# Every second output tile of an attention and gated-MLP kernel goes to the two tiles of the MLP's rectified values

## The chip, the cores and the metric

The kernel runs on one core of one Trainium2 chip. The metric is the device time of one execution in microseconds (us). Engines are named as in the profile: PE is TensorE's matmuls, PEld its weight loads, DVE is VectorE, ACT is ScalarE, POOL is GpSimd, SP is SyncE. A "q" behind a name is that engine's queue of issued instructions, for SP that of its transfers.

## What is computed

For 8 batches of 8 heads, attention with a decay over 576 positions of 64 values, and on its output (8 x 576 x 512) a gated MLP whose gate mixes positions:

```
decay  = cum[:, :, :, None] - cum[:, :, None, :]        # cum = cumsum(log(clip(f)))
attn   = softmax(where(causal, -1e9, q k^T / 8 + decay))
x      = (attn v), heads side by side                   # B x 576 x 512
h      = relu(x @ w_in);  u, v = h[..., :512], h[..., 512:]
v_n    = (v - mean(v)) / sqrt(var(v) + 1e-6)
gated  = u * (w_spatial @ v_n + b_spatial)              # over the 576 positions
out    = gated @ w_out                                  # B x 576 x 512
```

## The kernel before

The work is done in float32 precision on float32r operands: nearly every operand is kept as a high part and a rest, and a product is three (or two) matmuls. Attention (`attention`) goes through 32 pairs of heads, four to a batch; the MLP (`moe`) goes through the 8 batches. The main loop steps both generators side by side, attention a quarter of a batch and more ahead, so that a list of both in alternation is recorded. A scheduler that plans on modelled times then sets each engine's own order; every engine runs its list in order. A change that shifts one instruction can therefore shift everything planned behind it.

A batch of the MLP has these stages. For five groups of tokens (L532 to L570): sum `ps` of 12 matmuls, relu to the tile `vx` (L556, two buffers), mean and variance, the normalised value (L561), its high part `vnh` (ACT) and rest `vnl` (POOL). Then (L574 to L585) eight sums to the tiles `u`. Then for two halves of the tokens (L589 to L612) four gate sums `ps<-sph,vnh`, `spl,vnh`, `sph,vnl`, each multiplied by `u` on DVE and split in `gh` and `gl`. After each half, two output tiles of 128 tokens (`w_out_tile`, L620); after every odd batch a fifth one, with the 64 last tokens of two batches.

`w_out_tile` sums 12 matmuls with `wo` to a `ps` tile, copies it to an SBUF tile and issues its transfer to memory (256 KB) on SP's queue, for the fifth tile half of it on ACT's:

```
tag, bufs = ("vx", 2) if b == B - 1 and nps[0] % 3 else ("o", 1)
o = (mo if tag == "vx" else m2[0]).tile([128, DM], F32, name="o", tag=tag, bufs=bufs)
...
    A.copy(o, ps)
for bb, tok, p0, np_ in dst:
    (A if p0 else SY).dma_start(out=out[bb, tok:tok + np_, :], in_=o[p0:p0 + np_, :])
```

The tag names the buffers that a tile takes in turn. There is one buffer "o", so a copy to it waits until the transfer of the tile before it has read it. "vx" has two. In the last batch (`b == B - 1`) two of three tiles take "vx" already. In the sums, `ps` has two accumulators (the last batch also takes those of attention's scores `sc` and transposes `tp`, two each), so the third sum waits until the first is copied or multiplied away.

SP's queue also carries the loads of attention: for each head of a pair six (L312 to L317, `ta` and `tb`), the values (L323) and the raw queries and keys (L287). In attention, score tiles `sc` (`qkt`) are read by DVE (L357, with the row minimum), exponentiated on ACT (L359), scaled on POOL (L370), transposed on PE to `tp` (L416, L429), and cast from there by ACT to `eh` (L405) and by DVE to the rest `el` (L406); `x` are the products with the values.

Of the kernel before, what the change touches and what calls it, by code (L numbers as in the profile page):

```python
# [38 lines left out]
def attn_gmlp_kernel(ctx: ExitStack, tc: tile.TileContext, qk, v, f, w_in, w_sp, b_sp, w_out, out):  # L39
# [7 lines left out]
    B = out.shape[0]  # L47
# [101 lines left out]
    def after(i, mark, wait=False):  # L149
        if mark in last:  # L150
            tc.add_manual_dep(i.ins, last[mark].ins.name, mybir.DependencyInfo(
                mybir.DependencyClass.Sync if wait else mybir.DependencyClass.NoSync,
                mybir.DependencyReason.DATA), reason="order")
# [117 lines left out]
    def mm(o, l, r, st, sp):  # L271
        last['mm'] = T.matmul(o, l, r, start=st, stop=sp)  # L272
        return last['mm']
# [247 lines left out]
    nps = [0]  # L521

    def acc(b):

        nps[0] += 1
        pool, tag = ((ps_m, "ps"), (PS["t"], "tp"), (PS["s"], "sc"))[nps[0] % 3 if b == B - 1 else 0]
        return pool.tile([128, DM], F32, name=tag)

    def moe(b):
# [59 lines left out]
        for t0, nt in HALVES:  # L589
            gh, gl = [], []  # L590
            for j in range(NJ):
                ps = acc(b)
                o = ps[:, 0:nt]
                js = slice(128 * j, 128 * j + 128)
                for c in range(NB):
                    mm(o, vh[c][:, js], sph[c][:, t0:t0 + nt], c == 0, False)
                    mm(o, vh[c][:, js], spl[c][:, t0:t0 + nt], False, False)
                    mm(o, vl[c][:, js], sph[c][:, t0:t0 + nt], False, False)
                    yield 370
                mm(o, vh[NB][:, js], spta[:, t0:t0 + nt], False, False)  # L600
                mm(o, vb_[:, js], sptb[:, t0:t0 + nt], False, True)
                yield 246
                g = us[j, t0][:, 0:nt]
                V.tensor_tensor(out=g, in0=o, in1=g, op=ALU.mult)
                gh.append(m2[0].tile([128, 320], F32R, name="gh", tag="GH", bufs=3))
                gl.append(m2[0].tile([128, 320], F32R, name="gl", tag="U", bufs=9))
                A.copy(gh[j][:, 0:256], g[:, 0:256])  # L607
                G.tensor_tensor(out=gl[j][:, 0:256], in0=g[:, 0:256], in1=f32(gh[j][:, 0:256]), op=ALU.subtract)  # L608
                if t0:
                    th, tlo = (gt[0][:, r, j, r0:r0 + 64] for r in range(2))  # L610
                    A.copy(th, g[:, 256:320])
                    G.tensor_tensor(out=tlo, in0=g[:, 256:320], in1=f32(th), op=ALU.subtract)  # L612
            for c0 in (0, 128):
                yield from w_out_tile(b, [g[:, c0:c0 + 128] for g in gh], [g[:, c0:c0 + 128] for g in gl],
                                      [(b, t0 + c0, 0, 128)])
        if b % 2 == 1:
            yield from w_out_tile(b, *[[gt[0][:, r, j, :] for j in range(NJ)] for r in range(2)],
                                  [(b - 1, TL, 0, 64), (b, TL, 64, 64)])

    def w_out_tile(b, ghi, glo, dst):  # L620
        ps = acc(b)
        n = 0
        for j in range(NJ):
            for l, r in ((ghi, 0), (ghi, 1), (glo, 0)):
                i = mm(ps, l[j], wo[j][:, r, :], n == 0, n == 3 * NJ - 1)
                n += 1
                if b == B - 1 and n > 6:
                    after(i, "last")
            yield 648
        tag, bufs = ("vx", 2) if b == B - 1 and nps[0] % 3 else ("o", 1)  # L630
        o = (mo if tag == "vx" else m2[0]).tile([128, DM], F32, name="o", tag=tag, bufs=bufs)
        last["last"] = i
        if b == B - 1 and len(dst) == 1:
            V.tensor_copy(o, ps)
        else:
# [3 lines that stand above are left out]
# [94 lines left out]
```

## Time and profile before

| | |
|---|---|
| Median of 3 runs | 787.94 us (785.98 to 788.37) |
| The profiled execution | 786.43 us, of which the profile's span is 784.6 us |
| PE, PEld busy | 771.4 us (98%), 699.8 us (89%) |
| DVE, ACT, POOL busy | 553.1, 541.3, 470.9 us |
| DMA | 103.48 MB in 41713 packets |
| Output tiles | 40 transfers of them, 32 copies on ACT, 4 on DVE |

A row of the timeline reads: start and length in us, engine, line of the program, operation, output tile <- input tiles, shapes, number of instructions merged (x2), and in brackets the idle time of the engine just before it with what ended it. The waits table gives for each pair of engine, tile and line: us in total, times, the longest. PE's matmuls overlap, so a row's length is not the distance to the next one.

### The profile page before, as it was taken

The page shows a single profiled execution, that of the slowest core. Times are in us where ns is not written, and L with a number is a line of the kernel's source. Part 1 is how long each engine was busy: PE and PEld are TensorE (multiplying, and loading weights), DVE is VectorE, ACT ScalarE, POOL GpSimd, SP SyncE. Part 2 cuts the span into 40 slices and gives each one's busy share as a digit, 9 for nine tenths or more (in the row PEclk, how much of TensorE's full clock was granted, in tenths as well). Part 3 has the DMA queues.
Part 4 walks back from the last instruction along what each step waited for, and adds up shares of the span by engine and source line. Part 5 has one row for each costly group of instructions (what it writes and reads, how often), then busy time and mean ns, then how long its engine had stood idle before and what let it go on. Part 6 is the DMA issues. An engine that isn't in the chain of part 4 may idle for free.

```text
span 784.6 us, 15517 instructions
## 1 busy us (share of the span) xinstructions
PE 771.4 (98%) x4979; PEld 699.8 (89%) x4979; DVE 553.1 (70%) x1668; ACT 541.3 (69%) x1444; POOL 470.9 (60%) x687
## 2 busy tenths in 40 slices
PE   9998999999999999999999999999999999999997
PEld 4777889898999889998999989989899989999996
DVE  7989798867677587676766767776677768764422
ACT  8898697766866577667776768766686767764431
POOL 4666787858744476664755666555766547643241
PEclk9999999999999999999999999999999999999999
DMA  9848654654536644564565544556444665320001
GB/s 248 230 147 207 180 160 114 152 148 131 121 92 163 181 124 121 125 161 132 126 147 140 155 132 100 147 148 170 127 108 106 158 171 146 82 64 14 28 1 68
DMA packets 41713, 103.48 MB, mean 132 GB/s; under 512 B 6831, under 2 KB 8879, under 8 KB 41568
## 3 DMA queue, kind: packets, MB, share of 16 engines
q1 hardware_dynamic: 41306, 101.96, 50.9%
q8 instruction: 40, 0.66, 0.4%
q10 hardware_dynamic: 326, 0.53, 0.2%
q14 instruction: 41, 0.34, 0.1%
HBM read 39.42 MB, written 10.68 MB: 64 GB/s over the span
## 4 chain that ended last, share of the span: by engine, by line
PE 90%; DVE 3%; DMA 2%; POOL 2%; ACT 1%; issue 1%; ACTq 0%; POOLq 0%; DVEq 0%
PE ps L272 46%; PE sc L272 17%; PE x L272 13%; PE tp L416 9%; PE tp L429 2%; PE tp L272 2%; DMA out_dram<-o 2%; DVE tt L357 1%; POOL vnl L564 0%; DVE el L406 0%; ACT o L636 0%; POOL lo L292 0%; DVE xl L467 0%; DVE xl L465 0%; DMA ft<-in_dram 0%
## 5 line engine op out<-in xcount | busy, mean ns | idle before, releaser
L370 POOL TENSOR_SCALAR tt<-tt,sm 128x128 f32<-128x128 f32 (+1 forms) x228 | 126.5, 573 | 89.2 <-DVE sm L363 75.3
L357 DVE CUSTOM_DVE_ANT_0 tt<-sc,zm 128x128 f32<-128x128 f32 (+3 forms) x256 | 123.0, 485 | 71.5 <-PE tp L416 48.2
L405 ACT CAST eh<-tp 128x512 fp32r<-128x512 f32 (+1 forms) x270 | 112.4, 424 | 78.1 <-PE tp L416 41.4
L359 ACT ACTIVATE tt<-tt,nm 128x128 f32<-128x128 f32 (+3 forms) x256 | 144.4, 565 | 21.0 <-DVE nm L357 19.7
L406 DVE TENSOR_TENSOR el<-tp,eh 128x512 fp32r<-128x512 f32 (+1 forms) x270 | 129.1, 486 | 39.3 <-ACT eh L405 37.2
L416 PE MATMUL tp<-ident,tt 128*128 128x128 f32 x640 | 113.4, 278 | 0.8 <-DVE el L406 0.6
L292 POOL TENSOR_TENSOR lo<-raw,hi 128x320 fp32r<-128x320 f32 (+1 forms) x112 | 95.3, 881 | 26.0 <-ACT hi L290 25.3
L272 PE MATMUL sc<-ta 128*128 128x128 f32 (+1 forms) x336 | 107.6, 326 | 1.8 <-DVE wa L169 0.9
L272 PE MATMUL sc<-tb 68*128 68x128 f32 (+1 forms) x336 | 104.7, 318 | 2.0 <-DVE ef L401 1.3
L272 PE MATMUL x<-eh,vt 128*128 128x320 f32 (+4 forms) x378 | 105.1, 288 | 0.1
L272 PE MATMUL ps<-xh,win 128*128 128x256 f32 (+1 forms) x464 | 99.1, 301 | 0.0
L608 POOL TENSOR_TENSOR gl<-u,gh 128x256 fp32r<-128x256 f32 x64 | 47.8, 748 | 82.6 <-ACT gh L607 82.3
L272 PE MATMUL x<-el,vt 128*128 128x256 f32 x324 | 92.1, 303 | 0.0
L272 PE MATMUL ps<-win,xh 128*128 128x512 f32 x296 | 90.5, 396 | 0.0
L416 PEld LDWEIGHTS tp<-ident,tt 128*128 128x128 f32 x640 | 76.5, 141 | 8.2 <-PE sc L272 1.2
L272 PEld LDWEIGHTS ps<-xh,win 128*128 128x128 f32 x464 | 75.6, 189 | 0.5
L272 PEld LDWEIGHTS x<-eh,vt 128*128 128x128 f32 x378 | 71.0, 189 | 3.2 <-DVE xl L467 0.2
L272 PE MATMUL ps<-sph,vnh 128*128 128x256 f32 (+1 forms) x240 | 72.5, 302 | 1.3 <-ACT o L636 1.3
L272 PE MATMUL ps<-spl,vnh 128*128 128x256 f32 (+1 forms) x240 | 72.0, 300 | 0.0
L272 PE MATMUL ps<-sph,vnl 128*128 128x256 f32 (+1 forms) x240 | 71.2, 297 | 0.0
L272 PE MATMUL ps<-wo,gh 128*128 128x512 f32 x224 | 69.6, 401 | 1.0 <-ACT wo L178 1.0
L272 PEld LDWEIGHTS sc<-ta 128*128 128x128 f32 x336 | 63.7, 190 | 6.4 <-DVE nm L357 1.4
(177 smaller groups left out, 1898.1 us busy)
## 6 DMA issues: line engine op xcount, KB each, us to landing
raw<-in_dram SPq DMA_DIRECT2D x28, 608.0 KB
ta<-hi SPq DMA_DIRECT2D x56, 304.0 KB
vraw<-in_dram SPq DMA_DIRECT2D x32, 320.0 KB
tb<-hi SPq DMA_DIRECT2D x56, 160.0 KB
ta<-lo SPq DMA_DIRECT2D x56, 160.0 KB
out_dram<-o SPq DMA_DIRECT2D x32, 256.0 KB
ta<-hi SPq DMA_DIRECT2D x56, 144.0 KB
tb<-lo SPq DMA_DIRECT2D x56, 144.0 KB
```

The source lines that it names most:

```text
L272: last['mm'] = T.matmul(o, l, r, start=st, stop=sp)
L292: G.tensor_tensor(out=lo[:, c], in0=raw[:, c], in1=f32(hi[:, c]), op=ALU.subtract)
L357: V.tensor_tensor_reduce(out=t, in0=sc[:, 0:n], in1=zm[:, 640 - n:640], scale=-0.125, scalar=3.0e38, op0=ALU.add, op1=ALU.min, accum_out=n ...
L359: last["exp"] = last["exp", P, h, i] = A.activation(t, t, AF.Exp, bias=nm[:, i:i + 1], scale=-1.0, accum_out=se[:, i, 0:1])
L370: G.tensor_scalar(out=t, in0=t, scalar1=sm[:, i:i + 1], scalar2=1.0, op0=ALU.mult, op1=ALU.mult)
L405: A.copy(h_ap, ps)
L406: V.tensor_tensor(out=l_ap, in0=ps, in1=f32(h_ap), op=ALU.subtract)
L416: T.transpose(out=tp[:, (i - c) * 128:(i - c + 1) * 128], in_=tt[h][:, TOFF[i] + 128 * c:TOFF[i] + 128 * c + 128], identity=ident)
L429: T.transpose(out=tp[:, j * 128:(j + 1) * 128], in_=tl[:, c * 128:(c + 1) * 128], identity=ident)
L608: G.tensor_tensor(out=gl[j][:, 0:256], in0=g[:, 0:256], in1=f32(gh[j][:, 0:256]), op=ALU.subtract)
```

## The change

Ahead of the last batch, an output tile takes "vx" if the number of its token group (its first token by 128: 0 to 3, and 4 for the fifth tile) plus the number of the batch is even. So of the pairs of tiles in an even batch the first one goes to "vx" and the second to "o", in an odd batch the first to "o" and the second to "vx", and the fifth tile of an odd batch to "o". The last batch is as it was.

```
-        tag, bufs = ("vx", 2) if b == B - 1 and nps[0] % 3 else ("o", 1)
+        tag, bufs = ("vx", 2) if (nps[0] % 3 if b == B - 1 else (dst[0][1] // 128 + b) % 2 == 0) else ("o", 1)
```

Each engine has the same instructions as before. Up to the copy of the first output tile the orders are the same, then nearly all differ until the last batch's end. The first place is ScalarE at the first pair of output tiles of the third batch (b = 2): o_4785 and o_4844 are the two tiles, ps_4744 and ps_4788 their sums, eh the casts of transposed tiles, tt the exponentials. Before, around the second copy; the first one stands fourteen instructions ahead of it:

```order
L607 CAST gh_4871<-u_4311 128x256
L611 CAST gt_4532<-u_4311 128x64
L405 CAST eh_1231<-tp_4579 128x512
L359 ACTIVATE tt0_67,se2_99<-tt0_67,nm_4618 128x128
L464 CAST xh_4384<-x1_4515 64x320
L333 CAST vt_4560<-vraw_4558 128x5x2x64
L405 CAST eh_1231<-tp_4597 128x384
L359 ACTIVATE tt0_67,se2_99<-tt0_67,nm_4618 128x256
L636 COPY o_4844<-ps_4788 128x512
L516 CAST xh_4384<-xl_4385 128x64
```

And now, with both copies:

```order
L405 CAST eh_1231<-tp_4326 128x3x2x64
L405 CAST eh_1231<-tp_4335 128x2x2x64
L386 ACTIVATE tl_93,sm_4354<-tl_93,nm_4353 128x576
L636 COPY o_4785<-ps_4744 128x512
L636 COPY o_4844<-ps_4788 128x512
L405 CAST eh_1231<-tp_4431 128x512
L359 ACTIVATE tt1_68,se1_98<-tt1_68,nm_4468 128x128
L405 CAST eh_1231<-tp_4444 128x384
L464 CAST xh_4384<-x1_4387 64x320
```

The second copy has moved up to the first one, ahead of the casts and exponentials that stood between. On SP the two transfers of these tiles (rows `out_dram<-o`) stood behind the loads of both heads of the next pair, and now stand behind those of the first head alone.

The second place is TensorE in the same batch, at the sums to `u` (ps<-xh,win). sc_3952, sc_3974 and sc_4014 are score tiles, of which the third takes the accumulator of the first. Before:

```order
L272 MATMUL ps_4397<-xl_2731,win6_852 128x256
L272 MATMUL ps_4397<-xh_3063,win6_852 128x256 x2
L272 MATMUL ps_4397<-xl_3064,win6_852 128x256
L272 MATMUL ps_4397<-xh_3407,win6_852 128x256 x2
L272 MATMUL ps_4397<-xl_3408,win6_852 128x256
L416 MATMUL tp_3933<-ident_70,tt0_67 128x128
L272 MATMUL x0_4053<-eh_1231,vt_3882 128x256
L272 MATMUL x0_4053<-el_1232,vt_3882 128x256
L272 MATMUL x0_4053<-eh_1231,vt_3882 128x128
L272 MATMUL x0_4053<-el_1232,vt_3882 128x128
L272 MATMUL sc_4014<-ta_3885 128x288
L272 MATMUL sc_4014<-tb_3886 128x288
```

And now:

```order
L272 MATMUL sc_3952<-ta_3885 128x384
L272 MATMUL sc_3952<-tb_3886 128x384
L272 MATMUL sc_3974<-ta_3885 128x512
L272 MATMUL sc_3974<-tb_3886 128x512
L416 MATMUL tp_3925<-ident_70,tt0_67 128x128 x2
L272 MATMUL sc_4014<-ta_3885 128x288
L272 MATMUL sc_4014<-tb_3886 128x288
L272 MATMUL sc_4014<-ta_3893 128x288
L272 MATMUL sc_4014<-tb_3894 128x288
```

The sum ps_4397 (twelve products of 256 columns) and the products x0 that stood between sc_3974 and sc_4014 have gone elsewhere; two products and two transposes are left between the end of sc_3952 and its accumulator's next use.

## Rows read from the trace of the kernel before

**Rows 1.** The page, part 1 (busy us, share of the span, instructions of each engine), and of part 2 the granted clock of TensorE in 40 slices, in tenths of full speed (9 is 90% or more).

```profile
PE 771.4 (98%) x4979; PEld 699.8 (89%) x4979; DVE 553.1 (70%) x1668; ACT 541.3 (69%) x1444; POOL 470.9 (60%) x687
...
PEclk9999999999999999999999999999999999999999
```

**Rows 2.** The table by stretches, six from 160 to 753 us, of which two are shown: stretch, its length, busy us of PE, PEld, DVE, ACT and POOL (with instructions), granted clock, DMA share, GB/s; and the sum over all six.

```profile
330.00:350.00 20.00, 19.11 (x134) 18.23 (x134) 14.40 (x47) 15.29 (x44) 11.12 (x17) 1.00 0.70 176
...
520.00:530.00 10.00, 8.92 (x62) 8.42 (x61) 8.13 (x25) 7.44 (x23) 5.29 (x8) 1.00 0.57 143
...
sum 593.00, PE 590.87 PEld 551.47 DVE 409.91 ACT 403.65 POOL 349.07; mean PE 98.48 PEld 91.91 DVE 68.32 ACT 67.27 POOL 58.18
```

**Rows 3.** The table of waits over the whole span (who waited for whom: us in total, times, longest), and of the view of tile o the row of ACT's copies (ns: shortest, median, longest).

```profile
ACT eh L405 <- PE tp L416: 41.4, 47, 2.7
ACT o L636 <- DMA out_dram<-o: 23.0, 13, 3.6
PEld ps L272 <- ACT o L636: 1.7, 2, 0.9
PE ps L272 <- ACT o L636: 1.3, 2, 0.7
PE sc L272 <- DMA tb<-rows_d: 0.4, 1, 0.4
...
L636 ACT COPY o<-ps x32: 573/587/592, 151.6 to 780.4; 128x512 f32<-128x512 f32 x32
```

**Rows 4.** The timeline around the first pair of output tiles of the third batch: the longest of the loads on SP, the transfers, the two copies, and the next gate sum on PE. The transfers' row merges two, of which the first is issued at its start.

```profile
333.71 0.57 ACT L636 COPY o<-ps 128x512 f32<-128x512 f32 x1
...
334.85 1.17 SPq L314 DMA_DIRECT2D ta<-hi  x1
...
338.06 5.65 SPq L638 DMA_DIRECT2D out_dram<-o  x2
...
342.75 0.59 ACT L636 COPY o<-ps 128x512 f32<-128x512 f32 x1 [0.48 <-DMA out_dram<-o]
...
343.39 0.41 PE L272 MATMUL ps<-sph,vnh 128*128 128x320 f32 x1 [0.65 <-ACT o L636]
```

**Rows 5.** The timeline at the same place of the fifth batch: the gate sum's first product.

```profile
528.58 0.41 PE L272 MATMUL ps<-sph,vnh 128*128 128x320 f32 x1 [0.67 <-ACT o L636]
```

**Rows 6.** The timeline in the fourth batch, first pair: gate products on PE while ACT waits, and the second copy.

```profile
426.92 0.31 PE L272 MATMUL ps<-sph,vnl 128*128 128x320 f32 x1
...
427.06 0.31 PE L272 MATMUL ps<-spta,vnh 128*128 128x320 f32 x1
...
429.65 0.30 PE L272 MATMUL ps<-sph,vnh 128*128 128x320 f32 x1
...
429.80 0.31 PE L272 MATMUL ps<-spl,vnh 128*128 128x320 f32 x1
...
430.00 0.59 ACT L636 COPY o<-ps 128x512 f32<-128x512 f32 x1 [3.15 <-DMA out_dram<-o]
```

**Rows 7.** The timeline at the second pair of the fourth batch: a transfer's issue on SP, and the copy that waits for it.

```profile
448.59 0.37 SPq L638 DMA_DIRECT2D out_dram<-o  x1
...
451.21 0.59 ACT L636 COPY o<-ps 128x512 f32<-128x512 f32 x1 [0.97 <-DMA out_dram<-o]
```

**Rows 8.** The timeline at the second pair of the third batch: the copies, and the second relu of the next batch.

```profile
360.62 0.59 ACT L636 COPY o<-ps 128x512 f32<-128x512 f32 x1
...
364.83 0.59 ACT L636 COPY o<-ps 128x512 f32<-128x512 f32 x1 [0.53 <-DMA out_dram<-o]
...
368.78 0.61 ACT L556 ACTIVATE vx<-ps 128x512 f32<-128x512 f32 x1
```

**Rows 9.** The timeline around a score tile of 384 columns in the second batch: what follows its second product on PE (the first row starts as that product ends), and DVE's reading of it (two instructions).

```profile
262.95 0.28 PE L272 MATMUL x<-eh,vt 128*128 128x256 f32 x1
...
263.07 0.38 PE L416 MATMUL tp<-ident,tt 128*128 128x128 f32 x2
...
263.21 0.36 PE L272 MATMUL x<-el,vt 128*128 128x256 f32 x1
...
263.41 0.39 PE L272 MATMUL sc<-ta 128*128 128x512 f32 x1
...
263.49 0.56 DVE L357 CUSTOM_DVE_ANT_0 tt<-sc,zm 128x384 f32<-128x384 f32 x1 [0.22 <-PE tp L416]
...
263.88 0.23 PE L272 MATMUL x<-eh,vt 128*128 128x128 f32 x1
...
263.97 0.09 DVE L357 DVE_READ_ACCUMULATOR2_ANT nm<- 128x1 f32 x1
```

**Rows 10.** The groups of instructions by line and shape: two neighbouring kinds of product of one shape (busy us, mean ns of one, idle before).

```profile
L272 PE MATMUL x<-eh,vt 128*128 128x320 f32 x162 | 51.5, 324 | 0.1
L272 PE MATMUL x<-el,vt 128*128 128x320 f32 x162 | 49.8, 315 | 0.0
```

**Rows 11.** The chain of waits in order of time: start, us, what; the pieces that are transfers of output tiles, the longest ones.

```profile
263.19 3.69 DMA out_dram<-o
268.30 3.49 DMA out_dram<-o
...
338.06 4.62 DMA out_dram<-o
...
523.18 4.69 DMA out_dram<-o
```

## The prediction

> **What bounds the kernel now.** I read the engines' busy times first. TensorE is busy for 771.4 of 784.6 us, no other engine for more than 553.1, and its granted clock is at full speed in every slice [rows 1]. Then the table by stretches, because a mean hides where the rest lies. From 160 us, shortly after the first two output tiles, to 753 us, TensorE is busy for 590.87 of 593.00 us [rows 2]: it is idle for 2.13 us, and nearly all of that lies in 330 to 350 us (0.89) and in 520 to 530 us (1.08). The rest of its 13.2 us of idle time lies in the start and the last 30 us, which the change doesn't reach. So TensorE's own list of work sets the end, and what a change of buffers can return is what stands idle in those two places.
>
> Third, the table of waits. ScalarE stands 23.0 us before 13 copies of output tiles because the one tile "o" is still being written to memory; but TensorE waits for such a copy only twice, 1.3 us by its matmuls and 1.7 us by its weight loads [rows 3]. Fourth, the instructions around one of the two places [rows 4]. The first copy of the pair ends at 334.28. Its transfer to memory is issued at 338.06, since SP first works through six loads of attention's, the longest of them 1.17 us. The second copy starts at 342.75, and TensorE, which has no accumulator free for the next gate product, starts that at 343.39 after 0.65 us of idle time. The same pattern gives 0.67 us at 528.58 [rows 5]. Elsewhere the wait is longer and costs nothing: before 430.00 ScalarE waits 3.15 us, and TensorE's gate products follow each other every 0.15 us through all of it [rows 6].
>
> **The change part by part.**
>
> What it removes. The second copy of a pair no longer waits for the first one's transfer. No instruction is added or taken away: the copies stay 32 on ScalarE of 587 ns (median) [rows 3], the transfers keep their number and size, and TensorE's matmuls are the same. Of the 23.0 us of ScalarE's waiting, the two places are on the path, with the 1.7 us by which weight loads wait there [rows 3]. The other eleven waits I cost at nothing. What hides them is TensorE's other work, which is attention's products for the pairs ahead; if that cover were gone (it is in the last batch, whose tiles the change leaves as they are) they would cost up to 3.6 us each. The bounds of this term: at least 1.3 us (by the matmuls' waits), at most 2.13 us, TensorE's whole idle time from 160 to 753 us. **Term 1: -1.7 us.**
>
> That gain hangs on a slow transfer. From its issue to the next copy's start a transfer takes 4.69 us in the place at 338.06, and 2.62 us at 448.59 [rows 4, 7]. The Trainium skill, page "DMA: Bandwidth & Descriptors", section on the two cost components, says that a transfer costs about 2 us fixed and then its bytes at 436 GB/s; for these 256 KB that is an estimate of 2.6 us. It agrees with the quicker row and not with the slower one; were all transfers like that, the second copy would be ready 2.1 us earlier, there would be no stall to remove, and the sum would end 1.7 us higher. The stall is measured, so I keep the rows.
>
> What it moves. The copies of a pair now stand side by side on ScalarE and the transfers side by side on SP, mostly ahead of the second set of loads instead of behind it. The casts behind them (eh) start up to 0.59 us later. Their cover is large: ScalarE itself waits 41.4 us for TensorE before those casts [rows 3], so I cost this at nothing, which is the end that these rows are nearest to; the far end, 13 x 0.59 = 7.7 us with the cover gone in every place, belongs to the slower rival below. For SP, a load that stands behind a transfer must now wait for the copy; the bound from the trace is the one wait of TensorE for such a load, 0.4 us [rows 3]. I take nothing, as loads that stood behind the first transfer now stand behind two that are ready together.
>
> What it adds: a wait on the tile "vx". The two buffers alternate, and the first relu of the next batch takes the buffer that was free, the second takes the one that the last such output tile used. The tightest boundary is from an even batch. In batch 2 the copy that will use vx is the one at 360.62 and the second relu comes at 368.78, 8.16 us later; the hold lasts until the transfer is through, at 364.8, or 4.2 us after the copy's start [rows 8]. So 4 us are to spare and I cost it at nothing. In the slow place of [rows 4] the hold was 9.0 us, which would leave ScalarE waiting 0.9 us at three such boundaries, 2.6 us together, and TensorE has a second accumulator to cover it.
>
> What it does beside this: after the first pair of output tiles nearly every engine's order is another one, as the scheduler plans on from there. TensorE's list has the same matmuls in other places, and some stand closer to what they wait for. The place shown above in the order: a score tile (288 columns) follows the one of 384 columns that used its accumulator after only two products of 512 columns and two transposes. By the trace those take 0.47 + 0.14 us, and from the end of a 384-column score product (262.95) to the end of VectorE's reading of it (264.06) pass 1.11 us [rows 9]: 0.5 us short. The next tightest place that I found is short by some 0.2 us. Before, the first of them had twelve products of 256 columns and more in between. **Term 2: +0.7 us.** Bounds: 0 (VectorE's reading may come earlier, as it sat idle only 0.22 us there) and one such stall of 0.5 us in each of the seven batches that move, 3.5 us.
>
> **The sum.** The profiled execution took 786.43 us, its span 784.6 us. 786.43 - 1.7 + 0.7 = 785.4 us. That execution is 1.5 us below the median of the runs (787.94 us), so in terms of the median the forecast is **786.9 us**, a change of -0.13%. About 0.3%, 2.4 us, is what a measurement of this kernel can tell from no change. With the bounds of both terms the forecast's own range is 787.94 - 2.13 = 785.8 to 787.94 - 1.7 + 3.5 = 789.7 us.
>
> **The rivals.**
>
> *Denser products.* TensorE's rows overlap (a product of 320 columns is shown as 0.31 us and the next one starts after 0.15 us), so that short stalls hide inside "busy". With another order some 3800 products could each follow a little more closely. A mere 1 ns each gives 3.8 us, hence 787.94 - 1.7 - 3 = 783.3 us with most of that. For it: products of one form differ in mean by 9 ns between neighbours in the order (324 and 315 ns) [rows 10]. Against it: the scheduler's order was not made for that, and the number of changes between kinds of products is nearly the same in both orders. Chance 0.21.
>
> *The waits at face value.* The chain of waits passes four times through a transfer of an output tile, 3.69 + 3.49 + 4.62 + 4.69 = 16.5 us [rows 11]. If that time came back, 787.94 - 16.5 = 771.4 us would be left. The Trainium skill speaks for looking this way: its page "Perfetto Trace Analysis", section on the most-contended engine, calls TensorE's busy share a poor measure of the room that is left and wants the busy share of weight loads instead. That share is 89% here [rows 1], which by that page leaves room. What speaks against it in this trace is [rows 6]: during the longest such waits the products come at their usual distance, and a chain that runs through a transfer says nothing of TensorE's other work at that moment. Chance 0.05.
>
> *Accumulators turned over too fast* (slower). The place is score tiles and transpose tiles on TensorE in the new order, the mechanism that of term 2: products planned before VectorE or ScalarE have emptied the accumulator, which in-order TensorE can't pass. At 0.5 us each it decides from nine places on (9 x 0.5 - 1.7 = 2.8 us). With two in each of seven batches it is 7.0 us, thus 787.94 - 1.7 + 7.0 = 793.2 us. For it: the order shows more pairs of score tiles close to each other than before, and VectorE and ScalarE are busy for some 70% of the time [rows 1]. Against it: I found two such places, not nine. Chance 0.19.
>
> That the change does nothing is not a case: the order shows the copies side by side.
>
> **How the numbers follow.** Forecast 0.55 (within 0.3%), faster 0.21 + 0.05 = 0.26, slower 0.19. The range from 783.3 to 790.3 takes in the forecast, most of the denser order and the mild part of the slower rival; it leaves out the waits at face value and the 793 us end.
>
> **What would show it.** Right: no wait of ScalarE's copies for a transfer but a rest of a few us, where an odd batch's fifth tile uses "o" again; no idle TensorE before the gate product in the third and fifth batch; TensorE idle between 160 and 753 us for 1 to 3 us in other places, after score or transpose tiles; a relu's wait for a transfer absent. Wrong: a span shorter by over 2.4 us with the same idle time would speak for denser products; idle TensorE of over 4 us behind VectorE's reading of scores for the slower rival; relus that wait for a transfer would mean that I misjudged the hold of "vx".

## The result: slower by one per cent, and the profile after

The changed kernel takes 794.64 us (median of 6 runs, 792.83 to 796.58), the kernel before 786.56 us beside it (6 runs, 784.87 to 788.37): a ratio of **1.0102, 95% interval 1.0078 to 1.0126**, 8.1 us slower. The forecast was no change. Times of all kernels below are medians; ratios are to the kernel before, timed beside each on the same chip. The profiled executions of two kernels (a_ob and rev_parity, below) were disturbed ones, and nothing is read from their traces.

The profiled execution after took 794.53 us, its span 792.7 us. Part 1 of its page, and the clock of part 2:

```profile
PE 777.1 (98%) x4978; PEld 702.1 (89%) x4979; DVE 553.6 (70%) x1668; ACT 542.8 (68%) x1444; POOL 469.2 (59%) x687
...
PEclk9999999999999999999999999999999999999999
```

Against [rows 1] TensorE is busy for 5.7 us more with the same work, and the total of VectorE, ScalarE or GpSimd has moved by 1.7 us at most. A slice of part 2 is 19.8 us long, so that its 9 can hide a fall of the clock that lasts a few us. The table by stretches, from 160 us to where the same work ends in this order (761 us); columns as in [rows 2]:

```profile
160.00:330.00 170.00, 169.08 (x1125) 156.36 (x1124) 118.62 (x369) 118.67 (x320) 102.93 (x158) 1.00 0.52 130
330.00:350.00 20.00, 20.00 (x139) 19.31 (x138) 13.67 (x41) 12.52 (x37) 12.65 (x22) 1.00 0.63 154
350.00:386.00 36.00, 35.42 (x215) 31.23 (x214) 26.24 (x85) 25.36 (x66) 22.09 (x37) 1.00 0.60 150
386.00:396.00 10.00, 8.47 (x52) 8.14 (x51) 7.24 (x21) 7.21 (x19) 5.61 (x9) 0.83 0.39 89
...
570.00:590.00 20.00, 19.16 (x136) 17.48 (x136) 16.03 (x50) 16.07 (x42) 15.62 (x24) 1.00 0.71 171
...
sum 601.00, PE 596.60 PEld 553.62 DVE 411.61 ACT 407.20 POOL 348.64; mean PE 85.23 PEld 79.09 DVE 58.80 ACT 58.17 POOL 49.81
```

The place that the forecast was about is repaired: 330 to 350 us has no idle TensorE (0.89 us in [rows 2]). New idle time lies elsewhere, 4.40 us in all; the largest part is in 386 to 396 us (1.53 us), where the mean granted clock is 0.83 besides. The table of waits says the same:

```profile
ACT eh L405 <- PE tp L416: 61.4, 62, 2.8
...
PE sc L272 <- DMA tb<-rows_d: 3.4, 2, 2.2
...
ACT o L636 <- DMA out_dram<-o: 2.1, 1, 2.1
PE sc L272 <- DVE nm L357: 2.1, 4, 0.7
...
PE tp L416 <- DVE el L406: 1.7, 3, 0.8
```

ScalarE's copies wait 2.1 us for transfers instead of the 23.0 us of [rows 3], and no copy holds TensorE up any more. TensorE waits instead for loads of attention's operands (3.4 us, of which 2.15 us lie at 69.68 us, in the start, before the orders part, and 1.29 us at 388.19), for VectorE's reading of scores and for its differences el. The last two rows of before, in the same view:

```profile
PE sc L272 <- DVE nm L357: 0.7, 1, 0.7
...
PE tp L416 <- DVE el L406: 0.6, 1, 0.6
```

Those one-time waits of before lie in the start and are there after, too; the five new ones add 2.5 us. Two of them, the first at the place that the forecast had named:

```profile
300.06 0.40 PE L272 MATMUL sc<-ta 128*128 128x288 f32 x1 [0.55 <-DVE nm L357]
...
579.25 0.33 PE L416 MATMUL tp<-ident,tt 128*128 128x128 f32 x1 [0.77 <-DVE el L406]
```

Around 388 us, SP's queue and then TensorE:

```profile
378.01 0.33 SPq L287 DMA_DIRECT2D raw<-in_dram  x1
378.49 0.47 SPq L312 DMA_DIRECT2D ta<-hi  x1
...
380.75 1.60 SPq L315 DMA_DIRECT2D tb<-hi  x1
...
383.04 0.48 SPq L317 DMA_DIRECT2D tb<-rows_d  x1
```

```profile
386.61 0.30 PE L272 MATMUL sc<-ta 128*128 128x128 f32 x1 [0.24 <-DVE el L406]
...
388.19 0.30 PE L272 MATMUL sc<-tb 68*128 68x128 f32 x1 [1.29 <-DMA tb<-rows_d]
```

The raw queries and keys of a later pair (L287) are fetched just ahead of the six loads (L312 to L317) whose scores TensorE wants next. The first score waits a little (0.24 us, by the profile for VectorE), and the second for the last of the six, though that was issued 5.15 us earlier. In the old order the raw load stood behind these six.

### The profile page after: what moved, and what is told of

Read it like the earlier page. It is cut to its first block, busy times and chain, and to the rows that moved or that the text cites. A ratio compares the mean times of both kernels' runs of the same rounds, so it can differ in the third digit from the quotient of the medians.

```text
span 792.7 us, 15534 instructions
## 1 busy us (share of the span) xinstructions
PE 777.1 (98%) x4978; PEld 702.1 (89%) x4979; DVE 553.6 (70%) x1668; ACT 542.8 (68%) x1444; POOL 469.2 (59%) x687
## 4 chain that ended last, share of the span: by engine, by line
PE 88%; DVE 3%; POOL 3%; ACT 3%; DMA 2%; issue 1%; SPq 0%; POOLq 0%; DVEq 0%; ACTq 0%
PE ps L272 47%; PE sc L272 16%; PE x L272 12%; PE tp L416 8%; PE tp L272 2%; PE tp L429 2%; DMA tb<-rows_d 1%; POOL lo L292 1%; DVE tt L357 1%; ACT tt L359 1%; DVE el L406 1%; POOL tt L370 0%; DVE xl L465 0%; ACT eh L405 0%; DMA ft<-in_dram 0%
## 5 line engine op out<-in xcount | busy, mean ns | idle before, releaser
L357 DVE CUSTOM_DVE_ANT_0 tt<-sc,zm 128x128 f32<-128x128 f32 (+3 forms) x256 | 123.2, 486 | 87.7 <-PE tp L416 61.2
L405 ACT CAST eh<-tp 128x512 fp32r<-128x512 f32 (+1 forms) x270 | 112.1, 425 | 105.3 <-PE tp L416 61.4
L406 DVE TENSOR_TENSOR el<-tp,eh 128x512 fp32r<-128x512 f32 (+1 forms) x270 | 128.0, 485 | 26.0 <-ACT eh L405 24.4
L272 PE MATMUL ps<-xh,win 128*128 128x256 f32 (+1 forms) x464 | 100.7, 307 | 0.1
L272 PE MATMUL ps<-win,xh 128*128 128x512 f32 x296 | 92.7, 399 | 0.3 <-ACT vx L556 0.3
L272 PE MATMUL ps<-wo,gh 128*128 128x512 f32 x224 | 71.5, 404 | 0.9 <-ACT wo L178 0.9
```

What stands on the lines that cost most here:

```text
L357: V.tensor_tensor_reduce(out=t, in0=sc[:, 0:n], in1=zm[:, 640 - n:640], scale=-0.125, scalar=3.0e38, op0=ALU.add, op1=ALU.min, accum_out=n ...
L405: A.copy(h_ap, ps)
L406: V.tensor_tensor(out=l_ap, in0=ps, in1=f32(h_ap), op=ALU.subtract)
```

## Where the orders part, at equal work

Where both orders have issued the same set of matmuls, the start of the next one can be compared. I took this from two traces with the orders written out (b_ob, the kernel before, and a_oa, the changed one; below). The lead of the new order, in us, minus is ahead:

```
start in old order, us  152.9  159.8  201.5  284.7  320.9  377.3  388.7  526.8  561.4  659.6  738.5  end
new order behind, us     0.01  -1.53  -1.10  -0.26  +0.87  +0.63  +4.79  +4.22  +3.96  +6.55  +6.92  6.85
```

The first pair of output tiles gains 1.5 us, because in b_ob's trace TensorE waits there for the second copy (the first row is of its table of waits, the second of its timeline):

```profile
PE ps L272 <- ACT o L636: 1.2, 1, 1.2
...
157.64 0.41 PE L272 MATMUL ps<-sph,vnh 128*128 128x320 f32 x1 [1.21 <-ACT o L636]
```

The trace of the kernel before, which has the same order and buffers, has no wait at this place and has those at 343.39 and 528.58 us instead [rows 4, 5], which b_ob's lacks. So TensorE's waits for copies come to 1.3 and 1.2 us in the two executions, but not at the same places. All of the gain and more is then lost, in steps: 4.2 us between 377 and 389 us, some 2.6 us between 561 and 660 us, 1.1 us between 285 and 321 us. No stall in these three stretches is behind an output tile.

## Experiments

**The buffers and the order, one by one.** Each engine's instructions were chained to a written-out order by dependencies that carry no wait of their own, so that either order could be put on either kernel's buffers. What each of the four kernels adds, beside the table of its order:

```diff
+    pin(nc, tc)     # after the loop over the batches
+            tc.add_manual_dep(ins, prev.name, mybir.DependencyInfo(
+                mybir.DependencyClass.NoSync, mybir.DependencyReason.DATA), reason="pin")
```

b_ob: old buffers, old order.

> The kernel before, each engine's order written out as it is in the kernel before (no instruction moves): the control for the three others. Both theories: 786.6 us, ratio 1.000 within 0.002. Another time would say that writing the order out costs something by itself.

a_ob: new buffers, old order.

> The changed kernel's buffers (every second output tile in a tile of the rectified values), every engine in the order of the kernel before. Theory ORDER (the buffer is free, the new order costs): 784.5 to 786.6 us, ratio 0.997 to 1.000, the second copies' waits for their transfers gone and the TensorE stalls at 343 and 528 us with them. Rival BUFFER (the tile of rectified values that is taken, or the copies that now come back to back, delay other work): 792 to 796 us, ratio 1.007 to 1.012.

b_oa: old buffers, new order.

> The kernel before's single output tile, every engine in the order of the changed kernel. Theory ORDER: at least as slow as the changed kernel, 794 to 800 us, ratio 1.009 to 1.017 (the new order plus the second copies' waits, which stand behind no distance here). Rival BUFFER: 786 to 788 us, ratio 1.000 to 1.002.

a_oa: new buffers, new order.

> The changed kernel, each engine's order written out as it is in the changed kernel: the second control. Both theories: 794.6 us, ratio 1.008 to 1.013.

| | old order | new order |
|---|---|---|
| one tile "o" | 0.9999 (0.9986 to 1.0012) | 1.0661 (1.0635 to 1.0687) |
| every second in "vx" | 0.9992 (0.9975 to 1.0008) | 1.0109 (1.0085 to 1.0133) |

Writing the order out costs nothing, by both controls. The new buffers in the old order cost nothing either; their gain, 0.6 us, isn't separable from none. The whole loss comes with the order, and the BUFFER theory is refuted. b_oa was slower than I expected (839.15 us, not 794 to 800): an order in which the copies of a pair stand side by side is made for two tiles, and with one tile TensorE waits for output copies 13 times, 28.6 us in all and up to 5.1 us at a time, and the mean granted clock of the trace is 0.979 (0.997 in a_oa).

**One row of SP's queue.** In the new order with the new buffers:

```diff
-L287 DMA raw<-in_dram 128x1216
 L312 DMA ta<-hi 64x1216
 ...
 L317 DMA tb<-rows_d 4x1216
+L287 DMA raw<-in_dram 128x1216
```

> The changed kernel's buffers and order with one row of SP's queue moved: the load of the next pair's raw queries and keys (L287) goes behind, no longer ahead of, the six loads of ta and tb that TensorE waited for at 386.17 and 387.81 us (0.85 + 1.53 us over the normal spacing, and then 3.41 us of granted clock 0.5, some 1.7 us more). Theory ORDER (this place alone is 4.1 of the 6.9 us between the two orders): 2 to 4 us less than the changed kernel, 790.5 to 792.5 us, ratio to the kernel before 1.005 to 1.008. Rival CLOCK (the granted clock falls at any of these stalls, wherever): the stalls go, the fall comes elsewhere, 792.5 to 793 us. Rival NO PLACE (the loss is spread, and a removed stall comes back at the next wait): 794 to 795 us.

Measured 791.47 us, **1.0070 (1.0058 to 1.0082)**: 3.1 us of the loss (1.0109 less 1.0070, with the two intervals some 1 to 5 us) hang on this one row. In its trace the loads are issued faster, and the scores follow without a wait:

```profile
378.21 0.47 SPq L312 DMA_DIRECT2D ta<-hi  x1
...
380.31 0.73 SPq L315 DMA_DIRECT2D tb<-hi  x1
...
381.79 0.66 SPq L317 DMA_DIRECT2D tb<-rows_d  x1
382.50 0.64 SPq L287 DMA_DIRECT2D raw<-in_dram  x1
```

```profile
385.89 0.23 PE L272 MATMUL sc<-ta 128*128 128x128 f32 x1
385.96 0.27 PE L272 MATMUL sc<-tb 68*128 68x128 f32 x1
```

At equal work the two traces differ by 2.4 us in the two stalls and by 1.4 us in the products right behind, which run at a lower clock in a_oa (last section). NO PLACE is refuted here by the time, and CLOCK by the trace, in which the granted clock is 1.00 in every stretch of 2 us.

**Five pieces of TensorE's order.** Each stalled piece was moved behind the first 3 to 6 products that followed it; one of the five:

```diff
 L416 MATMUL tp<-ident,tt_67 128x128 x2
-L272 MATMUL sc<-ta 128x288
-L272 MATMUL sc<-tb 128x288     (both twice)
 L272 MATMUL ps<-xh,win_773 128x256 x2
 ...
+L272 MATMUL sc<-ta 128x288
+L272 MATMUL sc<-tb 128x288
```

> The changed kernel's buffers and order with five pieces of TensorE's order moved behind the first 3 to 6 products that followed them: the scores at 299.17, 370.25 and 568.95 us (0.71, 0.75, 0.43 us behind the evacuation of their accumulator, L357), the transposes at 578.86 and 735.59 us (0.93 + 0.30 and 0.46 us behind L406). Theory ORDER: these 3.6 us go and some of it comes back with the pieces' own consumers, so 1.5 to 3.5 us less than the changed kernel, 791 to 793 us, ratio to the kernel before 1.006 to 1.009. Rival NO PLACE: 794 to 795 us.

> Both edits, the raw load moved on SP and the five pieces moved on TensorE. Theory ORDER: the sum of both gains, 787 to 790 us, ratio to the kernel before 1.001 to 1.005: most of the loss repaired with the changed kernel's order otherwise kept. Rival NO PLACE: 793 to 795 us.

Measured 794.95 us, 1.0113 (1.0098 to 1.0128), and with the raw load moved as well 794.13 us, 1.0102 (1.0089 to 1.0115): no gain, and worse than the raw load alone. My expectation failed; NO PLACE held for these pieces. The trace of r2_products_between shows why. The wait of 0.55 us for scores at this place became one of 1.15 us of the products for their own accumulator, which ScalarE (L585) hadn't emptied:

```profile
299.87 0.38 PE L416 MATMUL tp<-ident,tt 128*128 128x128 f32 x2
301.39 0.51 PE L272 MATMUL ps<-xh,win 128*128 128x256 f32 x2 [1.15 <-ACT u L585]
...
302.21 0.30 PE L272 MATMUL sc<-ta 128*128 128x288 f32 x1
```

On top of these five pieces the raw load's edit brings only 0.0011 (1.0113 less 1.0102, not clear of nothing), against 0.0039 by itself: its price isn't the same in every order.

**What stands ahead of the evacuations.** On top of r1_raw_later; one of three such places on ScalarE, and one of two on VectorE:

```diff
-L333 CAST vt<-vraw 128x5x2x64
-L405 CAST eh<-tp 128x384
+L405 CAST eh<-tp 128x384
+L333 CAST vt<-vraw 128x5x2x64
...
+L406 TENSOR_TENSOR el<-tp,eh 128x384
 L465 TENSOR_TENSOR xl<-x_7794,xh 64x320
-L406 TENSOR_TENSOR el<-tp,eh 128x384
```

> The kernel with the raw load moved behind the six loads, and on top of it the order of the two evacuating engines changed at the three places where the products could not cover: on ScalarE the cast eh (L405) goes ahead of the 0.73 us cast of values (L333) at 296.75, 368.26 and 576.83 us; on VectorE the reading of the 384-column scores (L357) goes ahead of the two differences xl (L465, L467) at 368.59 us, and the difference el (L406) ahead of the one at 577.72 us. Theory EVACUATION (the stalls come from what stands ahead of the evacuation in ScalarE's and VectorE's order): the stalls at 370.25 (0.75) and 578.86 us (0.93 + 0.30) shrink to 0.4 us together, the one at 299.17 (0.71, where VectorE itself waits for a transpose) stays: 1.6 us less than with the raw load alone, 789.8 us, ratio to the kernel before 1.004 to 1.006. Rival CADENCE (no engine's order alone helps, the accumulators are short): the stalls move by a product or two, 791.5 us, 1.007.

Measured 793.05 us, 1.0070 (1.0048 to 1.0093): the same as without. The interval reaches into EVACUATION's range (1.004 to 1.006), so the time alone doesn't decide; the trace speaks for CADENCE. The stall of the scores at 370 us shrank from 0.75 to 0.35 us as expected, but new waits for VectorE (L357) came at 387.86 and 388.53 us (0.17 and 0.24). The transposes' stall near 577 us shrank from 0.93 to 0.25 us over the normal spacing, but the product behind them then waited longer for ScalarE, 0.83 us instead of 0.27:

```profile
576.86 0.83 PE L416 MATMUL tp<-ident,tt 128*128 128x128 f32 x3
578.30 0.56 PE L272 MATMUL ps<-xh,win 128*128 128x320 f32 x2 [0.61 <-ACT u L585]
```

At these places three kinds of accumulators (scores, transposes, products) wait for the two engines at once, and in both traces shown here one kind waits less and the next one behind it stalls.

**The two halves.** Old order up to a point, new order behind it, and the reverse (the tables joined where, on every engine, both orders have issued the same instructions). Both have the new buffers:

> The changed kernel's buffers; every engine in the order of the kernel before up to the point that TensorE reaches at 388.67 us there (393.46 us in the changed order; up to it both orders have issued the same matmuls), and in the changed order from there on. Theory ORDER (the loss is made place by place): what the changed order loses behind that point, 6.85 - 4.79 = 2.1 us, and not what it loses ahead of it: 786.5 to 789 us, ratio to the kernel before 1.000 to 1.004. Rival WHOLE (the loss needs the whole order, a drift that builds up and has no place): 785.5 us or 794 us, not between.

> The other half: the changed order up to that point, the order of the kernel before from there on, with the changed kernel's buffers. Theory ORDER: the 4.79 us that the traces show up to the point, or somewhat more, since both orders have the gain of the second tile in the first batch (1.5 us): 790 to 793 us, ratio to the kernel before 1.005 to 1.009. With the other half the losses over 785.45 us (these buffers in the old order) add up to that of the whole changed order, 9 us. Rival WHOLE: 785.5 or 794 us.

Measured 788.01 us, 1.0011 (0.9998 to 1.0024), and 791.72 us, 1.0056 (1.0036 to 1.0076). Both fall in their ranges. WHOLE is refuted by the second, which lies clear of both of its times; the first by itself can't be told from no loss. Over the new buffers in the old order (0.9992) the halves lose 0.0019 and 0.0064, together 0.0083, and the whole new order 0.0117. The rest of 0.0034 has an interval of some 0.004 either way, so the two may agree, and a part that needs the whole order isn't excluded. Each half's trace has the stalls of its own part of the new order: the first of these has TensorE waiting for nm, el and u at 562.54, 572.46 and 572.85 us (0.43, 0.93, 0.28), the second for nm and tb at 369.77 and 387.01 us (0.75, 1.67); these figures are over the normal spacing.

> The changed order with the raw load moved up to the point that TensorE reaches at 393.46 us, the order of the kernel before from there on. If the places add up: the half's ratio of 1.0056 less the raw load's 0.0039 (1.0109 less 1.0070), 1.0017, 788.5 us within 1 us. If the raw load's gain needs the second half: 1.0056, 791.7 us.

Measured 789.27 us, 1.0029 (1.0015 to 1.0043), within 1 us of the sum: the raw load's price (0.0027 here, 0.0039 before, each within some 0.0025) doesn't need the second half.

**SP's order alone.**

> The changed kernel's buffers, TensorE, VectorE, ScalarE and GpSimd in the order of the kernel before, SP's queue alone in the changed order. Theory ORDER: the raw load ahead of the loads costs where the first scores follow them closely, and at this place in the old order they come 10 us after the last of the loads: no stall there, 785 to 787.5 us, ratio 0.998 to 1.002. Rival QUEUE (SP's order is enough): 789 us and more, 1.003 and more, with TensorE waiting for tb near 388 us.

Measured 793.95 us, 1.0074 (1.0052 to 1.0096). My expectation failed. QUEUE's time held, though not for its reason: there is no stall for tb near 388 us. In this queue both transfers of a pair stand ahead of six loads, while TensorE still makes the second tile 8 us later. So the loads wait for the second copy's transfer, at 344.30 us, and TensorE for the loads (the first fence is SP's queue, the second TensorE):

```profile
344.30 0.34 SPq L638 DMA_DIRECT2D out_dram<-o  x1
344.73 0.47 SPq L312 DMA_DIRECT2D ta<-hi  x1
...
348.24 0.69 SPq L317 DMA_DIRECT2D tb<-rows_d  x1
```

```profile
349.37 0.40 PE L272 MATMUL sc<-ta 128*128 128x288 f32 x1 [1.31 <-DMA ta<-hi]
351.43 0.58 PE L272 MATMUL sc<-tb 68*128 68x288 f32 x1 [1.66 <-DMA tb<-rows_d]
```

The same loads start at 335.56 us in b_ob, before that copy. So a load behind a transfer is expensive where the copy is late; it is in this mixture, and not in the changed kernel, where both copies come at 334 us. Two more stalls follow, 1.41 us for a load of tb at 379.22 us and 1.10 us for a relu (L556) at 388.56 us.

**Other orders.** The change for batch 4 alone, and the change with the other tiles (those that had kept "o" take "vx", and the reverse; 17 tiles instead of 14). The scheduler was free in both:

```diff
-else (dst[0][1] // 128 + b) % 2 == 0)
+else b == 4 and (dst[0][1] // 128 + b) % 2 == 0)     # only_batch4
+else (dst[0][1] // 128 + b) % 2 == 1)                # rev_parity
```

> The change for the fifth batch alone (its second of two output tiles takes a tile of the rectified values), the order again left to the scheduler: 34 fewer tiles of work change their buffer, but TensorE's order differs from the kernel before in some 1,800 lines of its listing, a third of what the whole change moves. Theory ORDER (the time is that of whatever order comes out, not of the number of tiles): 784 to 792 us, and the difference to the kernel before is made of TensorE stalls at places that have nothing to do with output tiles. Rival PROPORTION (each tile in a tile of the rectified values costs its share): one tile of five, 788.2 us, ratio 1.002, with the difference at the fifth batch's tiles.

(A slip in that text: it is two of the 14 tiles that keep the new buffer, the first of each pair of that batch; PROPORTION would then give 786.17 + 2/14 x 8.1 = 787.3 us.)

> The other output tiles change their buffer (the first of each pair in a tile of the rectified values, the second in the tile of its own), the order left to the scheduler, which gives a fourth order. Theory ORDER: another draw, 784 to 796 us, the sum of its own stalls; anything beyond 0.3% of the changed kernel's 794.6 us would show that which tiles are moved matters through the order alone. Rival BUFFER: the same number of tiles, the same time as the changed kernel, 794.6 us.

Measured 791.47 us, 1.0068 (1.0053 to 1.0083), and 793.86 us, 1.0079 (1.0054 to 1.0105). Two tiles cost as much as two thirds of the whole change, so PROPORTION is refuted; its trace has the stalls at 566.39 (nm, 0.44) and 576.30 us (el, 0.93) that the whole change has, and new ones at 622 and 670 us. The one at 622.56 us is behind an output copy (0.71 us), so not all of them are away from output tiles. rev_parity can't be told from the changed kernel, and tells ORDER and BUFFER apart no further.

**A version that is faster than both.** New buffers, old order, and the raw load moved behind the six loads at the two places of the old order that have it ahead (329.73 and 514.10 us in b_ob's trace); the edit is that of r1_raw_later.

> The changed kernel's buffers in the order of the kernel before, with SP's queue edited at two places: the raw load (L287) that stands ahead of six loads of ta and tb at 329.73 and 514.10 us goes behind them. In that order TensorE waits there for tb<-lo at 338.90 (0.44 us) and tb<-rows_d at 523.49 us (0.62 us). Theory ORDER: these 1.0 us go, 784 to 785 us, ratio to the kernel before 0.997 to 0.999, and the trace has no stall behind an output copy (L636) at 345 and 529 us. Rival: the loads are late for another reason (the DMA engines), the stalls stay, 785.5 us.

Measured 785.12 us beside 787.3 us, **0.9980 (0.9966 to 0.9994)**. It is faster than both kernels; from the new buffers in the old order (0.9992) it can't be told, so what the moved loads add isn't shown by the time. From 160 to 750 us TensorE is busy for all but 0.11 us of its trace:

```profile
160.00:750.00 590.00, 589.89 (x3946) 550.88 (x3945) 407.90 (x1247) 403.63 (x1084) 347.48 (x537) 1.00 0.50 125
```

The two stalls for loads are gone, and those behind the output copies are down to some 0.3 us over the normal spacing, without the idle time of [rows 4, 5]:

```profile
341.24 0.57 ACT L636 COPY o<-ps 128x512 f32<-128x512 f32 x1
341.87 0.41 PE L272 MATMUL ps<-sph,vnh 128*128 128x320 f32 x1
```

This row alone doesn't show the buffers' gain, since b_ob's trace, with one tile "o", has as little there (0.35 and 0.31 us over the normal spacing). What b_ob's trace has and this one lacks are the stall at the first pair (1.21 us) and those for the loads (0.32 and 0.51 us). No copy waits for a transfer any more.

## Why the prediction was wrong

- **What bounds the kernel** was right: where two orders are compared at equal work, the lead changes at TensorE's stalls and at falls of its clock. That the change doesn't reach the time ahead of 160 us was wrong: in b_ob's trace the first pair's copy holds TensorE up for 1.21 us, and it is gone with the new buffers.
- **Term 1 (-1.7 us)**: the mechanism was right, the two places were luck of one execution. TensorE's waits for copies come to 1.3 us in the trace before and to 1.2 us in b_ob's, at another place, and no trace of the changed kernel has one. As the prediction says, the gain hangs on a slow transfer: from its issue at the first pair to the second copy's start pass 4.37 us in b_ob's trace and 2.96 us in that of the kernel before. The estimate of 2.6 us by the Trainium skill's page "DMA: Bandwidth & Descriptors" is given there for transfers that GpSimd issues, and these are SP's. In the old order the buffers alone give -0.6 us, with an interval from -2.0 to +0.6 us that holds the term, and nothing as well.
- **The step that failed is "for SP I take nothing"**, bounded by the one wait of 0.4 us in [rows 3]. I looked at loads that stand behind a transfer. What cost was a load against a load: the raw load that the new order puts ahead of six others whose scores come soon. The term was 3.1 us (r1_raw_later, some 1 to 5). The row of 0.4 us was such a place already: in the old order, too, a raw load stands ahead of the loads that TensorE waited for there.
- **Term 2 (+0.7 us) was mis-sized.** Its own place came as forecast (0.55 us of waiting at 300.06 us, 0.5 forecast), but TensorE's new waits for VectorE's L357 and L406 add up to 2.5 us in five places, not to 0.7 in two. That is inside the bounds of 0 to 3.5 us, and the value was taken near their wrong end. I counted from the order by TensorE's products alone; what stands ahead of an evacuation on VectorE and ScalarE, and the transposes' accumulators, I did not count.
- **The rival "accumulators turned over too fast"** gave 793.2 us and the right sign. That its time was close is in part luck: there are five such places and not the nine from which it was to decide, and the largest single part is the loads.
- **Casts behind the copies and the hold of "vx" at nothing**: no run contradicts this. No relu waits for a transfer. ScalarE's wait for TensorE before the casts grew from 41.4 to 61.4 us, but the casts' delay was not tried apart from the order. The fifth tile's rest came as said, 2.1 us once.
- **Denser products**: not seen. The mean of the 320-column product with eh went from 324 to 319 ns, the one with el from 315 to 316 ns [rows 10], and the time rose. **The waits at face value**: of 23.0 us of ScalarE's waiting 20.9 are gone, and the kernel is slower; with all of them gone, in the best version, the gain is 0.2% and not 16.5 us. The rule that the Trainium skill gives on the page "Perfetto Trace Analysis", section on the most-contended engine, is about how close the matmuls are to their peak. The runs don't test it: the weight loads' busy share was 89% before and after.
- **A term that was missing** is the clock, which the profile before shows at full speed throughout. Its 1.4 us (a_oa against r1_raw_later) are a part of the raw load's price.

From the forecast's -1.0 us to the measured +8.1 us are 9.1 us. The raw load has 3.1 of them, term 2 another 1.8 (2.5 less 0.7), term 1 some 1.1 (1.7 less 0.6). About 3 us are left, which no run assigns to one place.

What stays open: what sets the remaining 0.7% of r1_raw_later is shown only as a set of stalls that move when one engine's order is edited, not as one cause; the old order has fewer of them. Why the scheduler's plan is worse with more freedom wasn't tried.

## What to carry to other kernels

Where a scheduler plans the order, a change of buffers is a change of order: separate the two by writing the old order out on the new buffers before judging either. In the new order, look first at what the queues do, a large load that isn't urgent ahead of small ones that are, and then at what each evacuating engine does ahead of an evacuation. Here, stalled pieces that were put behind other work handed their stalls to the next accumulator (five pieces, no gain). And read a small stall from more than one execution: the same order showed its waits for copies at different places in two of them.

## What the runs showed of the hardware

TensorE's granted clock fell to its lower level, 0.50 of full speed (1.2 instead of 2.4 GHz), for 3.41 us behind the stalls at 388 us. The changed kernel in stretches of 2 us (columns as above):

```profile
386.00:388.00 2.00, 0.66 (x5) 0.34 (x3) 1.65 (x6) 1.95 (x7) 1.76 (x2) 1.00 0.95 213
388.00:390.00 2.00, 1.81 (x12) 1.84 (x13) 1.01 (x5) 1.23 (x3) 0.01 (x1) 0.83 0.88 202
390.00:392.00 2.00, 2.00 (x9) 1.99 (x8) 1.77 (x4) 0.85 (x3) 0.94 (x1) 0.50 0.11 32
392.00:394.00 2.00, 2.00 (x14) 1.97 (x13) 1.01 (x4) 1.53 (x4) 2.00 (x5) 0.82 0.00 0
```

TensorE was busy for 0.66 of 2 us, and the clock fell some 1 us after it had work again. The same work takes 2.31 us at that clock (389.54 to 391.85 us in a_oa) and 1.31 us at full speed (r1_raw_later). In sp_order_alone TensorE was busy for 0.40 us between 349 and 351 us; the clock fell at 350.9 us, within the second stall, and stayed at 0.50 for 6.8 us. It doesn't fall behind every stall of this size: in s_after_then_before TensorE waited 1.67 us at the same place, and the clock stayed at full speed. In the start (near 70 and 110 us) it fell in some executions and not in others: near 110 us in b_ob's trace and not in that of the kernel before, which has the same order, and in the changed kernel's and not in a_oa's. Each such fall lasts some 3.4 us; as the clock is halved, an estimate of its price in a single trace is up to 1.7 us.

The issues behind a raw load can take longer, too: for the six loads SP needed 5.03 us in the changed kernel (378.49 to 383.52 us, 1.60 us of it for L315) and 4.24 us in r1_raw_later (378.21 to 382.45, 0.73 us for L315). It isn't the same issue each time: at this place in s_after_then_before all six took 4.65 us, and L315 0.63 us.
